# One decode block on one core: load buffers at multiples of 1 KB, w4 loaded in 2 KB runs, and the last row's probabilities spread in other banks

## The chip, the core and the metric

The kernel runs on one core of a Trainium2 chip. The core has five engines with queues of their own: TensorE (PE in the profile, with its weight loads as PEld), VectorE (DVE), ScalarE (ACT), GpSimd (POOL) and SyncE (SP), which here issues nearly all DMAs. Sixteen DMA engines move the data. The metric is the device time of one execution in microseconds (us); less is better.

## The reference

One new token for each of 8 batch rows (`x` is 8 x 512). Attention with 32 query heads over 8 K/V heads of 128 looks at the last 2048 cached positions; an MLP block follows. The token shifts of the block's mixer take in nothing but padding at a sequence length of 1, so w1 and w2 contribute nothing.

```python
q = (x_ln @ wq).reshape(B, 1, 32, 128)                 # 512 -> 4096
k, v = k_cache[:, :, 6144:, :], v_cache[:, :, 6144:, :]  # 2048 positions, each head used by 4 query heads
p = softmax(q . k * 128 ** -0.5)
h = x + (p . v).reshape(B, 1, 4096) @ wo               # 4096 -> 512
u = layernorm(h)                                       # input of the second block
h2 = h + u + gelu(layernorm(u) @ w3) @ w4              # 512 -> 1792 -> 512 (hs is zero for S = 1)
```

In bf16 K and V are 32 MB each; wq and wo are 4 MB each, w3 and w4 1.8 MB each.

## The kernel before, in words

**Loads.** SP issues, in a written order, wq, 16 loads of K and 16 of V (2 MB each, half a batch row: 4 heads x 2048 positions), wo in four parts, w3, and w4 in three parts (`load_k` to `load_w4`, lines 618 to 640; the order is the string of line 643). K and V have three buffers each (`knat`, `vnat`). A K load waits until the transposes of the load three before it are done, a V load until the P x V of the one three before it is done; SP's queue is in order, so a load that waits holds all behind it. In a partition a K or V load is one row of 16 KB, wo has rows of 8 KB, w3 four of 3.5 KB, and w4 pieces of 7, 6 and 1 KB: partition p holds rows 14p to 14p + 13 of w4, and the loads take 7, 6 and 1 of them (`W4_AT`, line 601).

The tiles in SBUF lie one behind the other in the order in which they are declared (lines 103 to 171).

**Attention.** 64 items, 8 per batch row. For each, PE transposes 16 blocks of K into one of two pairs of PSUM banks (`pe_T`, line 315); ScalarE copies the lower half and VectorE the upper half to `kT_sb` (`evict`, lines 323 and 325); PE multiplies with the queries (`pe_QK`, line 335) into `S_ps`, one bank for even rows and one for odd. The order of PE's work is that of the loop at line 517: item p is transposed, then the parts of softmax and P x V of earlier rows that `A_WORK` and `B_WORK` place there, then the product with the queries of item p - 2. `LAG` puts the late parts of row 6 four items later, close before those of row 7.

Per row b the softmax has five parts. `softmax_1` to `softmax_3` find the maximum (line 354 on VectorE, small transposes through the bank `sm`), and ScalarE takes the exponential (line 372). `softmax_4` transposes P and VectorE copies it to `PT_sb` (line 384). Then `widen(b, x)`, for x from 0 to 3, spreads P over 128 columns with one matmul into a bank (line 397) and masks the result into `pT_sb`: on VectorE with one product (line 410), or, for x in `ON_ACT` = (1, 3), on ScalarE with four instructions (line 407). Even x use the bank `o_rows`, odd x an `S_ps` bank that is free (`bank_of`, line 388); both banks are also those of P x V. `softmax_5` adds up the row sums (lines 414 and 416).

`pe_PV` (line 426) multiplies the masked P with half a row of V, first into `o_rows`, then into `S_ps`; ScalarE and VectorE write the result as a high and a low bf16 part (lines 432 and 433). `pe_O` (line 443) brings it to the heads' layout; `oX` and `oW` (lines 453 and 459) scale it into the columns of `oW`.

**The rest.** wo comes in two forms: `pe_wo_row` (line 472) puts 24 of the 32 parts as rows into K's fourth bank, split into a high and a low part by lines 478 and 479 and brought back by `pe_hr` (line 502); meanwhile `pe_wo` (line 493) adds the other 8 parts directly, four matmuls each. A normalisation follows (lines 548 to 556), then 56 matmuls with w3 (line 568: 16, then the matmul for the variance at line 574, then 40), whose weights are columns with a step of 14; a square root and a GELU on ScalarE, each behind a load of its table (lines 581 and 593); 56 matmuls with w4 (line 607) that wait for the three loads in turn; and the sum, a transpose and the store.

`Engine.op` records an instruction with its waits, `emit` writes them to the engine's queue in that order.

Of the kernel before, what the change touches and what calls it, by code (L numbers as in the profile page):

```python
# [6 lines left out]
dt = mybir.dt  # L7
# [13 lines left out]
NC = W // 128  # L21
F = 1792
FC = F // 128
KC = D // 128
EPS = 1e-5

KQ = 4
NQ = 2
NS = 4
# [4 lines left out]
NKT = 4  # L34
LQK = 2
NPB = 3
ON_ACT = (1, 3)
JW = 32
JP = 8
QW = H  # L40


# [30 lines left out]
def bass_sequential_preLN__sliding_block_cached__mixer_s_mlp__decode_kernel(  # L73
# [19 lines left out]
    NITEM = NB * G  # L93
# [3 lines left out]
    with es:  # L97
        sb = lambda shape, dtype, name: es.enter_context(nc.sbuf_tensor(name, shape, dtype))
# [5 lines left out]
        ident_f = sb([128, 128], dt.float32, "ident_f")  # L104
        ident_b = sb([128, 128], dt.bfloat16, "ident_b")
        turn_b = sb([128, 128], dt.bfloat16, "turn_b")
        own_f = sb([128, KQ], dt.float32, "own_f")
        rows_f = sb([128, 64], dt.float32, "rows_f")
        heads_f = sb([128, H], dt.float32, "heads_f")
        sel_l = sb([128, 128], dt.float32, "sel_l")  # L110
        sel_o = sb([128, NS, 64], dt.bfloat16, "sel_o")
        ones_f = sb([128, 128], dt.float32, "ones_f")

        wbig = sb([128, KC * H * DH], dt.bfloat16, "wbig")
        wq_v = wbig[:, :].rearrange("p (k n) -> p k n", k=KC)
# [2 lines left out]
        vnat = sb([128, NV, CQ * DH], dt.bfloat16, "vnat")  # L118
        w3_sb = sb([128, KC, F], dt.bfloat16, "w3_sb")
        w4_sb = sb([128, FC, D], dt.bfloat16, "w4_sb")  # L120
        half = sb([128, B], dt.float32, "half")
        scratch = sb([128, 2], dt.float32, "scratch")
        eps2 = sb([128, 1], dt.float32, "eps2")
# [17 lines left out]
        PT_sb = sb([128, 512], dt.bfloat16, "PT_sb")  # L141
# [33 lines left out]
        kbank = [kT_ps[i // 2][:, (i % 2) * 1024:(i % 2 + 1) * 1024].bitcast(dt.float32) for i in range(4)]  # L175
# [16 lines left out]
        def dma(eng, dst, src, sem, *waits):  # L192
            def f(e):
                e.dma_start(dst, src).then_inc(sem, 16)
            eng.op(f, *waits, inc=False)
# [108 lines left out]
        def V(m):  # L304
            return sem_v[m % NV], 16 * (m // NV + 1)
# [16 lines left out]
        def evict(i):  # L322
            e_lo[i] = AC.op(lambda e: e.activation(kT_sb[:, i % NKT, 0:W // 2], kT_ps[i % 2][:, 0:W // 2], ACT.Copy),  # L323
                            e_Tlo[i], e_QK.get(i - NKT))
            e_hi[i] = DV.op(lambda e: e.tensor_copy(kT_sb[:, i % NKT, W // 2:W], kT_ps[i % 2][:, W // 2:W]),  # L325
                            e_Thi[i], e_QK.get(i - NKT))
# [57 lines left out]
            e_PTs[b] = sm_dv(lambda e: e.tensor_copy(PT_sb[:, :], pT_ps), e_PT[b], e_wide.get((b - 1, KQ - 1)))  # L384

        free = {2: None}

        def bank_of(x):
            if x % 2:
                for at in range(2):  # L390
                    if at in free:
                        return at, S_ps[at]
            return 2, o_rows

        def widen(b, x):
            at, bank = bank_of(x)
            e_wide[b, x] = PE.op(lambda e: e.matmul(bank[:, :], wide[:, x, :], PT_sb[:, :], start=True, stop=True),  # L397
                                 e_PTs[b], free[at], e_wd)
            a = own_f[:, :]
            own = bass.AP(tensor=a.tensor, offset=a.offset, ap=[a.ap[0], [0, KQ], [1, KQ], [0, H]])  # L400
            v = lambda t: t.rearrange("p n (t x) -> p n t x", t=KQ)
            to = v(pT_sb[:, b % 2, :, :].rearrange("p (n x) y -> p x n y", x=KQ)[:, x, :, :])
            got = v(bank[:, :].rearrange("p (n y) -> p n y", n=KQ))
            waits = e_wide[b, x], e_PV.get(NQ * (b - 2) + NQ - 1), e_own
            if x in ON_ACT:
                for t in range(KQ):
                    e = AC.op(lambda e, t=t: e.activation(to[:, :, t, :], got[:, :, t, :], ACT.Copy,  # L407
                                                          scale=own_f[:, t:t + 1]), *waits)
            else:
                e = DV.op(lambda e: e.tensor_tensor(to, got, own, ALU.mult), *waits)  # L410
            e_pT[b, x] = free[at] = e

        def softmax_5(b):
            e_Lb[b] = sm_pe(lambda e: e.matmul(sm[:, LB], sel_l[:, :], lcol[:, b:b + 1], start=True, stop=True),
                            e_exp[b], e_sell)
            e_rL[b] = sm_dv(lambda e: e.reciprocal(rL[:, b:b + 1], sm[:, LB]), e_Lb[b])

        def pe_PV(m):
            b, q = divmod(m, NQ)
            at, bank = bank_of(q)  # L420
            to = (orow, qrow)[m % 2]

            def f(e):
                for n in range(NN):
                    u = n % 2
                    ins = e.matmul(bank[64 * u:64 * (u + 1), :],  # L426
                                   pT_sb[:, b % 2, n, :].rearrange("p (x q) -> p q x", q=NQ)[:, q, :],
                                   vnat[:, m % NV, n * 512:(n + 1) * 512], start=(n < 2), stop=(n >= NN - 2),
                                   tile_position=(0, 64 * u), skip_group_check=True)
                return ins  # L430
            e_PV[m] = PE.op(f, V(m), e_pT[b, KQ - 2], e_pT[b, KQ - 1], free[at])
            e_ohi[m] = AC.op(lambda e: e.activation(to[:, 0, :], bank[:, :], ACT.Copy), e_PV[m], e_O.get(m - 2))  # L432
            e_olo[m] = DV.op(lambda e: e.tensor_tensor(to[:, 1, :], bank[:, :], to[:, 0, :], ALU.subtract), e_ohi[m])  # L433
            free[at] = e_olo[m]
# [27 lines left out]
        hT_ps = S_ps[0]  # L462
        e_wo = []
        hrow = kbank[3]
        LAST = NB - 1
        NP = JW // JP

        def pe_wo_row(k):
            def f(e):
                for j in range(JP * k, JP * (k + 1)):  # L470
                    u = j % 4
                    ins = e.matmul(hrow[32 * u:32 * (u + 1), :], oW[:, j, :], wo_v[:, j, :],
                                   start=(j < 4), stop=(j >= JP * (NP - 1) - 4),
                                   tile_position=(0, 32 * u), skip_group_check=True)
                return ins
            e = PE.op(f, e_oW[LAST], (sem_wo[k], 16), e_hi[NITEM - 1])
            if k == NP - 2:
                e = AC.op(lambda e: e.activation(hr[:, 0, :], hrow, ACT.Copy), e)
                e_wo.append(DV.op(lambda e: e.tensor_tensor(hr[:, 1, :], hrow, hr[:, 0, :], ALU.subtract), e))

# [5 lines left out]
                return ins  # L486
            PE.op(f, free[0], X, e_idb)

        def pe_wo(k):
            def f(e):  # L490
                for j in range(JP * k, JP * (k + 1)):
                    for nb in range(KC):
                        ins = e.matmul(hT_ps[:, nb * B:(nb + 1) * B], wo_v[:, j, nb * 128:(nb + 1) * 128],
                                       oW[:, j, 0:B], start=False, stop=False, skip_group_check=True)
                return ins
            PE.op(f, (sem_wo[k], 16), e_oW[LAST])

        def pe_hr():
            def f(e):
# [10 lines left out]
        def quad(f, q):  # L510
            return lambda b: f(NQ * b + q)
        A_WORK = (((1, softmax_2), (2, softmax_3)), ((0, softmax_1),))
        B_WORK = (((3, softmax_4), (4, each(widen, 0)), (4, each(widen, 1)), (5, each(widen, 2)), (5, each(widen, 3)),
                   (6, softmax_5)),
                  ((6, quad(pe_PV, 0)), (7, quad(pe_PV, 1)), (7, quad(pe_O, 0)), (8, quad(pe_O, 1))))
        LAG = (0, 0, 0, 0, 0, 0, KQ, 0)
        for p in range(NITEM + 24):
            if p < NITEM:
                pe_T(p)
                evict(p)  # L520
            if p == 1:
                e_qblk = q_turn()
            for when in (0, 1):
                for b in range(NB):
                    x = p - (G * b + G - 1 + LQK)
                    for at, part in A_WORK[when]:
                        if x == at:
                            part(b)
                    for at, part in B_WORK[when]:
                        if x == at + LAG[b]:  # L530
                            part(b)
                if when == 0 and 0 <= p - LQK < NITEM:
                    pe_QK(p - LQK)
        pe_x()
        for k in range(NP - 1):
            pe_wo_row(k)
        pe_wo(NP - 1)
        pe_hr()


# [22 lines left out]
        def pe_w3(lo, hi, *waits):  # L563
            def f(e):
                for fc in range(lo, hi):
                    n, f = divmod(fc, FH)
                    for kc in range(KC):
                        ins = e.matmul(y_ps[n][:, f * B:(f + 1) * B],  # L568
                                       w3_sb[:, kc, :].rearrange("p (m k) -> p k m", k=FC)[:, fc, :],
                                       uT[:, kc * B:(kc + 1) * B], start=(kc == 0), stop=(kc == KC - 1))  # L570
                return ins
            return PE.op(f, *waits)
# [25 lines left out]
                                                       ALU.mult, ALU.add), e)  # L598

        z_ps = S_ps[1]  # L600
        W4_AT = (0, 7, 13, FC)
        for n, waits in enumerate(((e_gT[0], free[1]), (e_gT[1],), ())):
            lo, hi = W4_AT[n:n + 2]
            def pe_w4(e, lo=lo, hi=hi):
# [32 lines left out]

        def load_w4(n):
            lo, hi = W4_AT[n:n + 2]
            dma(SP, w4_sb[:, lo:hi, :], B_w4.rearrange("(p k) n -> p k n", k=FC)[:, lo:hi, :], sem_w4[n])  # L640

        turn = {"K": 0, "V": 0, "O": 0}
        for kind in "KQKK" + 9 * "VK" + "VKKVKVKVVOVOVOO":
# [47 lines left out]
```

## Time and profile before

| | |
|---|---|
| median of 3 timed runs | 197.82 us (197.47 to 197.85) |
| the profiled execution | 196.63 us |
| its span, first to last instruction | 195.3 us |
| PE busy, VectorE, ScalarE | 153.8, 94.7, 102.5 us |
| data moved | 79.46 MB, 407 GB/s over the span |
| granted clock of PE, mean | 0.975 |

All rows come from the one profiled execution. Times are from the span's start. In the list of groups a line gives the line of the kernel, engine, operation, tiles, sizes and count, then the busy time in us, the mean of one instruction in ns, and the idle time before them with what ended it. In tables of stretches the columns are: the stretch, its length, busy time (with count) of PE, PEld, DVE, ACT and POOL, the granted clock of PE, the busy share of the DMA engines, and GB/s. "To landing" is the time from the issue of a load to the last of its data. The chain of waits is followed back from the last instruction. Busy time of PE comes from modelled ends of matmuls.

### The profile page before, as it was taken

The numbers are of one execution on the slowest core, as the hardware profiler recorded it, in microseconds if no ns is written. First come the engines' busy times: TensorE is split into PE (matmuls) and PEld (weight loads), VectorE is DVE, ScalarE is ACT, GpSimd is POOL, SyncE is SP. The second block draws the span as 40 slices with busy tenths as digits, with TensorE's granted clock in tenths as the row PEclk, the third lists the DMA queues.
The fourth block names the chain that finished last, engine by engine and source line by source line (L and its number), as shares of the span: only waits on it lengthen the run. The fifth ranks groups of instructions, "written<-read, shape, count | busy, mean of one in ns | idle before, by whom it ended". The sixth has DMA issues, their size and how long they took to land.

```text
span 195.3 us, 4485 instructions
## 1 busy us (share of the span) xinstructions
PE 153.8 (79%) x1997; PEld 105.0 (54%) x2005; DVE 94.7 (48%) x196; ACT 102.5 (52%) x169; POOL 7.7 (4%) x16
## 2 busy tenths in 40 slices
PE   0002989997989798979897986969999997949675
PEld 0001667674657465646564664636766672525475
DVE  7700465654275437543754373527553747251241
ACT  3000568785458545864586355835784686351242
POOL 8300000000000000000000000000000000000012
PEclk9999999999999999999999999999999999997985
DMA  5999999999999999999999999999999999999980
GB/s 223 423 436 426 429 426 429 419 429 423 426 426 421 424 423 429 423 429 426 426 429 423 429 423 426 426 419 429 423 429 423 429 406 436 371 426 412 409 351 31
DMA packets 6370, 79.46 MB, mean 407 GB/s; under 512 B 712, under 2 KB 848, under 8 KB 1616
## 3 DMA queue, kind: packets, MB, share of 16 engines
q1 hardware_dynamic: 6336, 79.18, 96.3%
q8 instruction: 15, 0.25, 0.5%
q14 instruction: 3, 0.02, 0.0%
q10 hardware_dynamic: 16, 0.01, 0.0%
HBM read 79.18 MB, written 0.01 MB: 405 GB/s over the span
## 4 chain that ended last, share of the span: by engine, by line
DMA 51%; PE 37%; DVE 6%; ACT 3%; issue 1%; SPq 1%
DMA knat<-in_A_k_cache_dram 32%; PE kT_ps L315 14%; DMA vnat<-in_A_v_cache_dram 11%; DMA wbig<-in_A_wq_dram 8%; PE o_rows L426 5%; PE S_ps L335 4%; PE S_ps L426 4%; PE S_ps L268 2%; PE kT_ps L568 2%; ACT pT_sb L407 2%; PE S_ps L397 1%; PE sm L443 1%; DVE kT_sb L325 1%; DVE mcol L354 1%; PE S_ps L607 1%
## 5 line engine op out<-in xcount | busy, mean ns | idle before, releaser
L323 ACT ACTIVATE kT_sb<-kT_ps 128x1024 bf16<-128x1024 bf16 x64 | 65.9, 1032 | 32.7 <-PE kT_ps L315 32.5
L315 PE MATMUL kT_ps<-turn_b,knat 128*128 128x128 bf16 x1024 | 68.1, 220 | 10.9 <-DMA knat<-in_A_k_cache_dram 10.9
L315 PEld LDWEIGHTS kT_ps<-turn_b,knat 128*128 128x128 bf16 x1024 | 57.4, 98 | 26.3 <-DMA knat<-in_A_k_cache_dram 14.7
L325 DVE COPY kT_sb<-kT_ps 128x1024 bf16<-128x1024 bf16 x64 | 44.4, 694 | 37.6 <-PE kT_ps L315 36.8
L335 PE MATMUL S_ps<-kT_sb,qblk 128*32 128x512 bf16 x256 | 26.9, 390 | 0.7 <-DVE qblk L290 0.7
L407 ACT ACTIVATE pT_sb<-S_ps,own_f 128x128 bf16<-128x128 f32 x64 | 18.4, 388 | 3.4 <-PE S_ps L397 3.4
L426 PE MATMUL o_rows<-vnat,pT_sb 128*64 128x512 bf16 x128 | 17.0, 412 | 1.2 <-ACT pT_sb L407 1.2
L433 DVE TENSOR_TENSOR orow<-o_rows,orow 128x512 bf16<-128x512 f32 x8 | 5.5, 691 | 20.7 <-ACT orow L432 20.7
L426 PE MATMUL S_ps<-vnat,pT_sb 128*64 128x512 bf16 x128 | 15.3, 382 | 0.2 <-DMA vnat<-in_A_v_cache_dram 0.2
L433 DVE TENSOR_TENSOR qrow<-S_ps,qrow 128x512 bf16<-128x512 f32 x8 | 5.5, 691 | 15.0 <-ACT qrow L432 15.0
L335 PEld LDWEIGHTS S_ps<-kT_sb,qblk 128*32 128x32 bf16 x256 | 7.2, 93 | 9.2 <-issue 4.9
L426 PEld LDWEIGHTS o_rows<-vnat,pT_sb 128*64 128x64 bf16 x128 | 7.2, 117 | 8.2 <-issue 4.0
L432 ACT ACTIVATE orow<-o_rows 128x512 bf16<-128x512 f32 x8 | 4.8, 597 | 13.1 <-PE o_rows L426 13.1
L268 PE MATMUL S_ps<-wbig,xlnT 128*32 128x512 bf16 x32 | 3.6, 629 | 10.1 <-DMA wbig<-in_A_wq_dram 10.1
L432 ACT ACTIVATE qrow<-S_ps 128x512 bf16<-128x512 f32 x8 | 4.8, 597 | 12.7 <-PE S_ps L426 12.7
L410 DVE TENSOR_TENSOR pT_sb<-o_rows,own_f 128x512 bf16<-128x512 f32 x16 | 10.9, 680 | 0.5 <-PE S_ps L335 0.5
L426 PEld LDWEIGHTS S_ps<-vnat,pT_sb 128*64 128x64 bf16 x128 | 6.9, 111 | 7.0 <-issue 1.5
L274 ACT ACTIVATE qrow<-S_ps 128x512 bf16<-128x512 f32 x1 | 0.6, 597 | 17.2 <-PE S_ps L268 17.2
L397 PE MATMUL S_ps<-PT_sb,wide 128*128 128x512 bf16 x16 | 6.1, 381 | 2.3 <-DVE qrow L433 1.0
L268 PEld LDWEIGHTS S_ps<-wbig,xlnT 128*32 128x32 bf16 x32 | 1.2, 138 | 11.6 <-issue 11.6
L594 POOL TENSOR_SCALAR r<-vsum 128x8 f32<-128x8 f32 x1 | 0.2, 243 | 181.9 <-DVE vsum L578 181.9
L372 ACT ACTIVATE P_sb<-S_ps,negcol 128x512 bf16<-128x512 f32 x8 | 5.5, 687 | 2.3 <-DVE negcol L371 2.3
(98 smaller groups left out, 115.7 us busy)
## 6 DMA issues: line engine op xcount, KB each, us to landing
knat<-in_A_k_cache_dram SPq DMA_DIRECT2D x16, 2048.0 KB, 20.3
vnat<-in_A_v_cache_dram SPq DMA_DIRECT2D x16, 2048.0 KB, 20.0
wbig<-in_A_wq_dram SPq DMA_DIRECT2D x1, 4096.0 KB, 16.6
wbig<-in_A_wo_dram SPq DMA_DIRECT2D x4, 1024.0 KB, 15.7
w_sb<-in_B_w_dram SPq DMA_DIRECT2D x1, 1792.0 KB, 17.4
w_sb<-in_B_w_dram SPq DMA_DIRECT2D x1, 896.0 KB, 19.0
w_sb<-in_B_w_dram SPq DMA_DIRECT2D x1, 768.0 KB, 20.5
w_sb<-in_B_w_dram SPq DMA_DIRECT2D x1, 128.0 KB, 19.6
```

Source lines behind the costliest of these rows:

```text
L268: ins = e.matmul(S_ps[j][32 * u:32 * (u + 1), :], xlnT[:, kc, :], wq_v[:, kc, n:n + R * DH], start=(kc == 0), stop=(kc == KC - 1), tile_po ...
L315: ins = e.matmul(kT_ps[i % 2][:, n * 128:(n + 1) * 128], knat[:, j % NK, c * DH:(c + 1) * DH], turn_b[:, :], is_transpose=True)
L323: e_lo[i] = AC.op(lambda e: e.activation(kT_sb[:, i % NKT, 0:W // 2], kT_ps[i % 2][:, 0:W // 2], ACT.Copy), e_Tlo[i], e_QK.get(i - NKT))
L325: e_hi[i] = DV.op(lambda e: e.tensor_copy(kT_sb[:, i % NKT, W // 2:W], kT_ps[i % 2][:, W // 2:W]), e_Thi[i], e_QK.get(i - NKT))
L335: ins = e.matmul(S_ps[b % 2][32 * t:32 * (t + 1), :], qblk[:, b, KQ * q + t, at:at + H], kT_sb[:, i % NKT, :].rearrange("p (n t a) -> p t ...
L372: e_exp[b] = AC.op(lambda e: e.activation(P_sb[:, b % NPB, :], S_ps[j][:, :], ACT.Exp, bias=negcol[:, b:b + 1], scale=1.0, accum_out=lcol[ ...
L397: e_wide[b, x] = PE.op(lambda e: e.matmul(bank[:, :], wide[:, x, :], PT_sb[:, :], start=True, stop=True), e_PTs[b], free[at], e_wd)
L407: e = AC.op(lambda e, t=t: e.activation(to[:, :, t, :], got[:, :, t, :], ACT.Copy, scale=own_f[:, t:t + 1]), *waits)
L410: e = DV.op(lambda e: e.tensor_tensor(to, got, own, ALU.mult), *waits)
L426: ins = e.matmul(bank[64 * u:64 * (u + 1), :], pT_sb[:, b % 2, n, :].rearrange("p (x q) -> p q x", q=NQ)[:, q, :], vnat[:, m % NV, n * 512 ...
L432: e_ohi[m] = AC.op(lambda e: e.activation(to[:, 0, :], bank[:, :], ACT.Copy), e_PV[m], e_O.get(m - 2))
L433: e_olo[m] = DV.op(lambda e: e.tensor_tensor(to[:, 1, :], bank[:, :], to[:, 0, :], ALU.subtract), e_ohi[m])
```

## The change

Four small tiles (`own_f`, `sel_l`, `sel_o`, `ones_f`) are declared behind the load buffers instead of ahead of them. The rows of w4 are dealt out in groups of 256: in group g partition p holds rows 256g + 2p and 256g + 2p + 1, which lie side by side in memory; the three loads take 3, 3 and 1 groups. The columns of w3 are taken in the same order. Of each row's four blocks of P only block 1 is masked on ScalarE. For the last row (b = 7), blocks 0 to 2 go to the first three of K's banks. P x V waits for all four blocks. Before the last row's first P x V, `warm` puts four matmuls whose result nobody reads into K's fourth bank. Of wo, 20 parts instead of 24 go as rows.

```diff
+FG = FC // 2
-ON_ACT = (1, 3)
+ON_ACT = (1,)
+JR = 20
...
-        own_f = sb([128, KQ], dt.float32, "own_f")
-        sel_l = sb([128, 128], dt.float32, "sel_l")
-        sel_o = sb([128, NS, 64], dt.bfloat16, "sel_o")
-        ones_f = sb([128, 128], dt.float32, "ones_f")
         wbig = sb([128, KC * H * DH], dt.bfloat16, "wbig")
...
         w4_sb = sb([128, FC, D], dt.bfloat16, "w4_sb")
+        own_f = sb([128, KQ], dt.float32, "own_f")
+        sel_l = sb([128, 128], dt.float32, "sel_l")
+        sel_o = sb([128, NS, 64], dt.bfloat16, "sel_o")
+        ones_f = sb([128, 128], dt.float32, "ones_f")
...
-        def bank_of(x):
+        LAST = NB - 1
+        def bank_of(x, b=0):
+            if b == LAST and x < KQ - 1:
+                return 3 + x, kbank[x]
             if x % 2:
...
         def widen(b, x):
-            at, bank = bank_of(x)
+            at, bank = bank_of(x, b)
...
+        def warm(b):
+            def f(e):
+                for n in range(4):
+                    ins = e.matmul(kbank[KQ - 1], ident_b[:, :], PT_sb[:, :], start=True, stop=True)
+                return ins
+            if b == LAST:
+                PE.op(f, e_hi[NITEM - 1])
...
-            e_PV[m] = PE.op(f, V(m), e_pT[b, KQ - 2], e_pT[b, KQ - 1], free[at])
+            e_PV[m] = PE.op(f, V(m), *(e_pT[b, x] for x in range(KQ)), free[at])
...
-        def pe_wo_row(k):
+        def pe_wo_row(j0, j1):
             def f(e):
-                for j in range(JP * k, JP * (k + 1)):
+                for j in range(j0, j1):
                     u = j % 4
                     ins = e.matmul(hrow[32 * u:32 * (u + 1), :], oW[:, j, :], wo_v[:, j, :],
-                                   start=(j < 4), stop=(j >= JP * (NP - 1) - 4),
+                                   start=(j < 4), stop=(j >= JR - 4),
...
-                   (6, softmax_5)),
+                   (6, softmax_5), (6, warm)),
...
+            if p == NITEM - 1:
+                free[3], free[4], free[5] = e_lo[p - 1], e_hi[p - 1], e_lo[p]
...
-        for k in range(NP - 1):
-            pe_wo_row(k)
-        pe_wo(NP - 1)
+        for j in range(0, JR, JP):
+            pe_wo_row(j, min(j + JP, JR))
+        pe_wo(JR, NP * JP - JP)
+        pe_wo(NP * JP - JP, NP * JP)
...
-                                       w3_sb[:, kc, :].rearrange("p (m k) -> p k m", k=FC)[:, fc, :],
+                                       w3_sb[:, kc, :].rearrange("p (g m k) -> p g k m", g=FG, k=2)[:, fc // 2, fc % 2, :],
...
-        W4_AT = (0, 7, 13, FC)
+        W4_AT = (0, 6, 12, FC)
...
-            dma(SP, w4_sb[:, lo:hi, :], B_w4.rearrange("(p k) n -> p k n", k=FC)[:, lo:hi, :], sem_w4[n])
+            dma(SP, w4_sb[:, lo:hi, :].rearrange("p (g k) n -> p g (k n)", k=2),
+                B_w4.rearrange("(g p k) n -> p g (k n)", g=FG, k=2)[:, lo // 2:hi // 2, :], sem_w4[n])
```

More of the change, by code (lines that the diff above doesn't have):

```diff
@@ L464, in bass_sequential_preLN__sliding_block_cached__mixer_s_mlp__decode_kernel @@
         hrow = kbank[3]
-        LAST = NB - 1
         NP = JW // JP
-        def pe_wo_row(k):
+        def pe_wo_row(j0, j1):
             def f(e):
-                for j in range(JP * k, JP * (k + 1)):
+                for j in range(j0, j1):
                     u = j % 4
                     ins = e.matmul(hrow[32 * u:32 * (u + 1), :], oW[:, j, :], wo_v[:, j, :],
-                                   start=(j < 4), stop=(j >= JP * (NP - 1) - 4),
+                                   start=(j < 4), stop=(j >= JR - 4),
                                    tile_position=(0, 32 * u), skip_group_check=True)
                 return ins
-            e = PE.op(f, e_oW[LAST], (sem_wo[k], 16), e_hi[NITEM - 1])
-            if k == NP - 2:
+            e = PE.op(f, e_oW[LAST], (sem_wo[j0 // JP], 16), e_hi[NITEM - 1])
+            if j1 == JR:
                 e = AC.op(lambda e: e.activation(hr[:, 0, :], hrow, ACT.Copy), e)
@@ L487, in pe_x, with pe_wo @@
             PE.op(f, free[0], X, e_idb)
-        def pe_wo(k):
+        def pe_wo(j0, j1):
             def f(e):
-                for j in range(JP * k, JP * (k + 1)):
+                for j in range(j0, j1):
                     for nb in range(KC):
@@ L495, in f @@
                 return ins
-            PE.op(f, (sem_wo[k], 16), e_oW[LAST])
+            PE.op(f, (sem_wo[j0 // JP], 16))
         def pe_hr():
```

## The prediction

> **What bounds the kernel now.** I read the page first (span, slices, queues), then the chain of waits in order of time, then the stretches of the last 30 us, then the issues and their landings.
>
> ```profile
> span 195.3 us, 4485 instructions
> DMA  5999999999999999999999999999999999999980
> DMA packets 6370, 79.46 MB, mean 407 GB/s; under 512 B 712, under 2 KB 848, under 8 KB 1616
> q1 hardware_dynamic: 6336, 79.18, 96.3%
> ```
>
> The DMA engines are busy in every slice but the first and the last two. One queue carries 79.18 MB, so the data cannot arrive before about 190 us, whatever the other engines do. The chain (start, length, what) shows where compute still counts:
>
> ```profile
> 127.47 20.97 DMA vnat<-in_A_v_cache_dram
> 148.44 0.04 issue
> 148.48 1.92 PE S_ps L426 x16
> ...
> 163.23 1.15 ACT pT_sb L407 x4
> ...
> 166.52 1.85 PE o_rows L426 x16
> ...
> 171.96 0.41 PE S_ps L397
> 172.37 0.02 issue
> 172.39 1.15 ACT pT_sb L407 x4
> ...
> 174.01 1.15 ACT pT_sb L407 x4
> 175.16 0.14 issue
> 175.30 3.53 PE o_rows L426 x16
> 178.83 1.74 PE S_ps L426 x16
> ...
> 183.46 1.51 PE kT_ps L472 x24
> ...
> 187.68 1.12 PE kT_ps L568 x16
> ...
> 189.11 2.34 PE kT_ps L568 x40
> 191.46 1.58 PE S_ps L607 x56
> 193.04 0.02 issue
> ```
>
> Until 148.48 the chain hangs on loads; from there to the end it is compute alone. But the last loads run close beside it. These are issues of SP (start, length), then single loads (KB each, us from issue to landing), then the group of the four w3 and w4 issues (lengths, first and last start):
>
> ```profile
> 168.40 0.54 SPq L194 DMA_DIRECT2D vnat<-in_A_v_cache_dram  x1
> 170.09 2.78 SPq L194 DMA_DIRECT2D w_sb<-in_B_w_dram  x4
> ```
> ```profile
> vnat<-in_A_v_cache_dram SPq DMA_DIRECT2D x1, 2048.0 KB, 9.5
> w_sb<-in_B_w_dram SPq DMA_DIRECT2D x1, 1792.0 KB, 17.4
> w_sb<-in_B_w_dram SPq DMA_DIRECT2D x1, 128.0 KB, 19.6
> ```
> ```profile
> L194 SPq DMA_DIRECT2D w_sb<-in_B_w_dram x4: 473/532/1114, 170.1 to 172.4; - x4
> ```
>
> The last V lands at 168.40 + 9.5 = 177.9, and its matmuls start at 178.83: 0.9 us to spare. w3 lands at 170.09 + 17.4 = 187.5, and the w3 matmuls start at 187.68: 0.2 to spare. The last 128 KB of w4 land at 172.4 + 19.6 = 192.0; their 4 matmuls are the last of 56 that end at 193.04 with 1.58/56 = 0.028 us each, so they start near 192.8: 0.8 to spare, and the piece before (some 0.3 us earlier, 191.7) is needed after 28 of 56, at 192.25: 0.5 to spare. So compute ends the run, with three loads 0.2 to 0.9 us behind it. A gain in compute alone soon meets a load; a gain in the DMA stream moves everything.
>
> **The load buffers' addresses.** wbig, knat, vnat, w3_sb and w4_sb begin 544 bytes past a multiple of 1 KB in each partition (byte 20000 in the laid-out program) and now begin on one (18432): four small tiles (own_f padded to 32, and three of 512 bytes) are declared behind them. No instruction changes. Per DMA engine there are (6370 - 712)/16 = 354 descriptors with data. What one costs beyond its bytes comes from stretches with different sizes (30 to 150 us: 16 KB rows; 178 to 183: 8 KB and 3.5 KB rows; 18 to 26.5: 16 KB rows, early):
>
> ```profile
> DMA packets 3508, 51.07 MB, mean 426 GB/s; under 512 B 390, under 2 KB 390, under 8 KB 390
> ```
> ```profile
> DMA packets 400, 2.06 MB, mean 412 GB/s; under 512 B 25, under 2 KB 25, under 8 KB 245
> ```
> ```profile
> DMA packets 239, 3.65 MB, mean 430 GB/s; under 512 B 16, under 2 KB 16, under 8 KB 16
> ```
>
> First: 120 us x 16 / 3118 = 615 ns for 16.4 KB. Second: 5 x 16 / 375 = 213 ns for 5.5 KB. The slope is 36.9 ps per byte, which leaves some 10 ns a descriptor (rough, since a stretch cuts packets at its edges). Third: 8.5 x 16 / 223 = 610 ns. So 5 of the 10 ns come and go at unchanged addresses and are not alignment; at most the other 5 can be. Outer bound 354 x 10 ns = 3.5 us gained. Nothing in the rows names a loss, but nothing excludes one either: I allow 2.5 ns the other way, 0.9 us lost. I take half of the 5 ns: 354 x 2.5 = 0.9 us at the end of the stream, 0.8 where w3, V and the last K land. The Trainium skill (DMA: Bandwidth & Descriptors, How a descriptor splits into AXI transactions) has a descriptor that does not start at a multiple of 256 B begin at the boundary below and pay for the unused bytes; 544 past 1 KB is 32 past 256, one 32-byte beat, and by our own slope that estimate is 354 x 1.2 ns = 0.4 us. By that the run would come out at 197.1 instead of the 196.6 below. It also states (Advanced Engine Details and Errata, Clock Domains) that an unobstructed 1 KiB descriptor takes 42 to 43 ns; 1 KB at our slope is 38, so as an estimate 5 of the 10 ns would stay in any case. No run so far shows either.
>
> **w4 in 2 KB runs.** A partition's rows of 7, 6 and 1 KB become 3 + 3 + 1 pieces of 2 KB. Per engine 8 partitions x 3 = 24 descriptors become 56: +32 x 10 ns = 0.3 us, at the end of the stream, with nothing to hide it (bounds: 0 and, at twice the price, 0.6). SP still issues three loads. The chunks become 6, 6 and 2 rows of 128, so the last two land as 768 and 256 KB.
>
> Sum for the stream: the last landing moves from 192.0 to 192.0 - 0.9 + 0.3 = 191.4. The piece before lands 256 KB / 400 GB/s = 0.65 earlier, at 190.75; its 24 matmuls take 24 x 0.028 = 0.7 and end at 191.45; then 8 matmuls, 0.25, and about 0.15 until the result is out: 191.85 instead of 193.04. That is 1.2 us less, if compute is there by then.
>
> **The masks.** Of each row's four blocks, block 3 goes from ScalarE (1.15 us for its four instructions) to VectorE:
>
> ```profile
> L410 DVE TENSOR_TENSOR pT_sb<-o_rows,own_f 128x512 bf16<-128x512 f32 x16 | 10.9, 680 | 0.5 <-PE S_ps L335 0.5
> ```
>
> For rows 0 to 5 this adds 0.68 us to VectorE per row of some 20 us, and the copies of K behind it wait; the loads set the pace there, so I cost it at nothing (without that cover, 0.7 a row). For row 6 it stands on the path. VectorE's queue has mask 2 (to 164.9), now mask 3 (to 165.6), and only then the reduce of Mrow, on which the lcol matmul, the reciprocal and the first P x V of row 6 wait through the shared bank sm. That P x V began at 166.52; it slips by about 0.4. For row 7 the blocks 0 to 2 go to K's banks, idle after the last copy, so they no longer wait for the S bank and for each other: the chain 171.96, 172.39, 173.59, 174.01 goes. Next late is VectorE: mask 0 to 172.9, then oX and oW of row 6 (they follow the O matmuls of row 6, which wait for orow/qrow), then masks 2 and 3, ending near 175.1. Against 175.16 + 0.14 that is 0.15 less in all. PE's new wait on all four blocks ends with the same mask; behind it on PE stands nothing but the rest of the tail. The V load of SP that waits for row 6's first P x V is issued 0.4 later, behind several us of other loads (landing 9.5 us after issue against 4.9 for 2 MB at 426 GB/s): free.
>
> **Four extra matmuls (warm).** The rows of PE's clock (us, busy of PE, PEld, DVE, ACT, POOL, clock, DMA share, GB/s):
>
> ```profile
> 172.00:174.00 2.00, 1.66 (x13) 1.02 (x13) 1.51 (x4) 1.14 (x4) 0.00 (x0) 1.00 1.01 422
> 174.00:176.00 2.00, 0.79 (x5) 0.42 (x7) 0.38 (x2) 1.14 (x4) 0.00 (x0) 0.80 0.94 401
> 176.00:178.00 2.00, 2.00 (x12) 0.99 (x10) 0.00 (x0) 0.00 (x0) 0.00 (x0) 0.50 1.00 422
> ```
>
> Row 7's first P x V runs at half clock: 3.53 us against 1.85 for row 6's. Four matmuls of 512 columns (about 0.9 us) now stand where PE waited for masks. If they hold the clock, that P x V ends 1.7 earlier, at 177.0; but the last V lands at 177.9, less 0.8. So of 1.7 about 1.0 + 0.8 is usable at best, and if the clock falls anyway nothing is lost, since PE waited there.
>
> **wo.** Row form takes 20 instead of 24 (1.51 x 4/24 = 0.25 less); the other form gets 48 matmuls instead of 32, about 1.3 us, under the 1.3 us that ScalarE and VectorE need for the rows' two halves (bounds: 0 and +0.3 outside).
>
> **w3 in steps of 2.** Step 14 cost 1.12/16 = 0.070 and 2.34/40 = 0.058 us a matmul; w4's contiguous weights cost 0.028. What step 2 costs no row shows: between. Only the first 16 matter, since the rest lie beside ScalarE's table load: 0 to 0.65 us less, I take 0.3.
>
> **Sum of the compute side.** Last V lands at 177.9 - 0.8; P x V, wo and norm follow as before, less 0.25, so uT is ready at 187.6 - 1.7 - 0.25 = 185.7 (warm works) or about 186.5 (it does not). w3 lands at 187.5 - 0.8 = 186.7: it decides in both cases, so warm, masks and wo vanish behind it. The w3 matmuls start 1.0 earlier, and w4's, 0.3 more, at 190.15; 24 of them end at 190.8, when the second piece is there (190.75). So the stream ends the run: 191.85, a gain of 1.2 us, of which 0.9 - 0.3 is the stream's own and 0.6 is slack behind w4 that the compute side gives up. The profiled execution took 196.63, below all three timed runs; I subtract from their median: 197.82 - 1.2 = 196.6. The measurement tells 0.2% (0.4 us) from no change.
>
> **Rivals.**
> *Alignment gives nothing.* For it: the rate of 426 GB/s varies with time, not with address. Then the last landing is 192.3, the result 192.75: 0.3 less, 197.5, within 0.2%. Chance 0.19.
> *Alignment gives most of the 10 ns*, say 7. Then 2.5 us of the stream go: the last landing is 189.8, which allows 190.25, 2.8 less. Compute has to follow: the V at 148.44 comes 354 x 148/190 x 7 ns = 1.9 earlier, masks and wo give 0.4, w3's step 0.3, and a clock that falls gives no more: 2.6 less, 195.2. Against it: the 5 ns that vary at fixed addresses. Chance 0.14.
> *w4's small pieces hold the end up.* The 1.8 MB of w4 now take 4.5 us (187.5 to 192.0). In 2 KB pieces they may move at 310 GB/s as against 400: +1.2 us. With no gain from alignment the last landing is 193.2, the result 193.65: 0.6 slower, 198.4. It decides once w4's stretch grows by over 0.6 us more than alignment saves. For it: they are the smallest data descriptors in number; against it: the 10 ns. Chance 0.13, with all other ways to lose.
> *Warm fails.* Half clock again at 176 to 178: as worked out, the time stays within 0.1 of the forecast as long as w3 decides.
>
> **How the numbers follow.** The forecast (alignment saves 0.4 to 2 us of stream) has 0.54 and its own range 195.6 to 197.4. Faster by over 0.2%: 0.54 + 0.14 = 0.68; same 0.19; slower 0.13. The range for 8 in 10 reaches from the large gain to the small loss: 195.1 to 198.2.
>
> **What would show it.** Right: stretch 30 to 150 at 428 GB/s or more; w3 landing before 187, and the w3 matmuls starting with that landing; the w4 matmuls waiting for a load; clock 1.00 at 176 to 178. Wrong: the same 426 GB/s (alignment is nothing), a last w4 landing after 192.5 (the small pieces), PE waiting for a mask beyond 175.5, or w3 matmuls still at 0.06 us.

## The result, and the profile after

Six timed runs of each: 195.67 us median (194.42 to 196.36) against 197.64 (197.18 to 198.29). The ratio is 0.9891 with a 95% interval of 0.9849 to 0.9933: 2.2 us faster. The prediction said 196.6, between 195.1 and 198.2.

The page of the changed kernel, the lines that answer to those shown of before:

```profile
span 194.9 us, 4506 instructions
DMA  5999999999999999999999999999999999799990
DMA packets 6883, 79.47 MB, mean 408 GB/s; under 512 B 712, under 2 KB 720, under 8 KB 2128
q1 hardware_dynamic: 6848, 79.18, 95.9%
```

512 more packets are w4's small pieces. The same bytes move, but one slice of the DMA line near the end, at about 166 to 170.5 us, now shows a gap. The profiled execution (196.35 us) is one of the two longest of the six. Its stretch from 30 to 150 us:

```profile
DMA packets 3538, 51.51 MB, mean 429 GB/s; under 512 B 393, under 2 KB 393, under 8 KB 393
```

120 us x 16 / 3145 = 610.5 ns for a 16 KB descriptor, against 120 x 16 / 3118 = 615.8 before. The chain of waits (start, length, what):

```profile
126.39 20.85 DMA vnat<-in_A_v_cache_dram
147.24 0.04 issue
147.29 1.92 PE S_ps L439 x16
...
165.82 3.55 PE o_rows L439 x16
169.38 0.55 PE sm L382 x4
169.93 0.02 SPq L196
...
172.06 0.60 SPq L196
172.66 0.04 issue
172.71 18.62 DMA w_sb<-in_B_w_dram
191.33 0.04 issue
191.38 1.03 PE S_ps L622 x32
192.41 0.02 issue
```

The V load on which the tail's chain hangs lands at 147.24 instead of 148.44: 1.2 us gained by then. At the end the w4 matmuls wait for a piece of w4, as forecast, but it lands at 191.33 and not at 190.75. But between the two the gain is lost again: row 6's first P x V takes 3.55 us, at half clock, where it took 1.85, and SP's last loads wait for it. Stretches of the changed kernel, columns as before (the clock, the DMA share and GB/s are the last three):

```profile
164.00:166.00 2.00, 1.14 (x6) 0.98 (x8) 1.06 (x5) 0.00 (x0) 0.00 (x0) 0.73 0.96 410
166.00:168.00 2.00, 2.00 (x12) 0.82 (x10) 0.02 (x1) 0.78 (x2) 0.00 (x0) 0.50 0.99 422
168.00:170.00 2.00, 2.00 (x14) 0.75 (x12) 0.00 (x0) 0.58 (x1) 0.00 (x0) 0.50 0.51 209
170.00:172.00 2.00, 2.00 (x12) 0.85 (x12) 1.02 (x2) 0.02 (x1) 0.00 (x0) 0.56 0.79 295
176.00:178.00 2.00, 1.62 (x15) 0.82 (x14) 0.81 (x3) 0.00 (x0) 0.00 (x0) 1.00 0.95 389
```

Between 168 and 172 the DMA engines move 209 and 295 GB/s: they have run dry. Against 429 that is 2 x (220 + 134)/429 = 1.65 us of stream lost. The half clock has moved from row 7 (before: 0.50 at 176 to 178) to row 6.

### The profile page after: what moved, and what is told of

Read it like the earlier page. It is cut to its first block, busy times and chain, and to the rows that moved or that the text cites. A ratio compares the mean times of both kernels' runs of the same rounds, so it can differ in the third digit from the quotient of the medians.

```text
span 194.9 us, 4506 instructions
## 1 busy us (share of the span) xinstructions
PE 155.2 (80%) x2021; PEld 104.1 (53%) x2021; DVE 98.9 (51%) x204; ACT 94.7 (49%) x137; POOL 7.7 (4%) x16
## 4 chain that ended last, share of the span: by engine, by line
DMA 61%; PE 30%; DVE 5%; SPq 2%; issue 1%
DMA knat<-in_A_k_cache_dram 32%; PE kT_ps L317 14%; DMA vnat<-in_A_v_cache_dram 11%; DMA w_sb<-in_B_w_dram 10%; DMA wbig<-in_A_wq_dram 9%; PE S_ps L337 4%; PE o_rows L439 4%; PE S_ps L439 2%; SPq L196 2%; PE S_ps L270 2%; DVE mcol L356 1%; DVE kT_sb L327 1%; PE sm L456 1%; DVE pT_sb L415 1%; DVE qblk L292 1%
## 5 line engine op out<-in xcount | busy, mean ns | idle before, releaser
L439 PE MATMUL S_ps<-vnat,pT_sb 128*64 128x512 bf16 x128 | 16.3, 399 | 0.2 <-DMA vnat<-in_A_v_cache_dram 0.2
L415 DVE TENSOR_TENSOR pT_sb<-o_rows,own_f 128x512 bf16<-128x512 f32 x14 | 9.5, 682 | 0.5 <-PE o_rows L402 0.5
L412 ACT ACTIVATE pT_sb<-S_ps,own_f 128x128 bf16<-128x128 f32 x28 | 8.0, 375 | 1.2 <-PE S_ps L402 1.2
L278 DVE TENSOR_SCALAR qrow<-S_ps 128x512 bf16<-128x512 f32 x1 | 0.7, 691 | 11.7 <-PE S_ps L270 11.7
## 6 DMA issues: line engine op xcount, KB each, us to landing
w_sb<-in_B_w_dram SPq DMA_DIRECT2D x1, 1792.0 KB, 15.2
w_sb<-in_B_w_dram SPq DMA_DIRECT2D x1, 256.0 KB, 16.5
```

The lines of the kernel that those rows point to most:

```text
L439: ins = e.matmul(bank[64 * u:64 * (u + 1), :], pT_sb[:, b % 2, n, :].rearrange("p (x q) -> p q x", q=NQ)[:, q, :], vnat[:, m % NV, n * 512 ...
```

## The experiments

Times are ratios to runs of the kernel before on the same chip, with a 95% interval. Where a profile's execution may not be typical, the spans of all timed executions are named beside it.

**The parts, one at a time.** Alignment alone: the kernel before, with four declarations moved.

```diff
-        own_f = sb([128, KQ], dt.float32, "own_f")   # and sel_l, sel_o, ones_f
...
         w4_sb = sb([128, FC, D], dt.bfloat16, "w4_sb")
+        own_f = sb([128, KQ], dt.float32, "own_f")   # and sel_l, sel_o, ones_f
```

> The kernel before with only the four small tiles moved behind the load buffers, so that these begin at multiples of 1 KB. Theory A (the stream of loads sets the time and alignment shortens it): the stretch 30 to 150 us runs at 429 GB/s or more instead of 426, the last w4 load lands 1.3 to 1.7 us earlier, and the time falls by 1.0 to 1.6 us, since w3 and w4 had only 0.2 to 0.8 us to spare and the compute chain starts from a V load that comes 1.1 us earlier. Theory B (the gain is the tail's compute: masks, warm, w3): the loads land earlier but the time falls by less than 0.5 us.

Measured: 0.9926 (0.9889 to 0.9962), 1.5 us faster (0.8 to 2.2); the median of its spans is 194.25 us, that of the kernel before beside it 196.1. Its stretch from 30 to 150 us, its last load with its issues, and two pieces of its chain:

```profile
DMA packets 3540, 51.51 MB, mean 429 GB/s; under 512 B 395, under 2 KB 395, under 8 KB 395
```
```profile
w_sb<-in_B_w_dram SPq DMA_DIRECT2D x1, 128.0 KB, 18.7
```
```profile
L194 SPq DMA_DIRECT2D w_sb<-in_B_w_dram x4: 444/490/1343, 168.8 to 171.2; - x4
```
```profile
167.09 9.26 DMA vnat<-in_A_v_cache_dram
176.38 1.94 PE S_ps L426 x16
```

The last w4 load lands at 171.2 + 18.7 = 189.9 instead of 192.0: 2.1 us earlier, where 1.3 to 1.7 were expected. In this execution PE waits for the last V (176.4). Theory A holds, and most of the gain, 1.5 of 2.2 us, is alignment's.

Everything but the alignment: the changed kernel with the four declarations back in their old place (the diff above, reversed).

> The changed kernel with the four small tiles put back ahead of the load buffers, so everything but the alignment. Theory A: within 0.5 us of the kernel before (at most the 0.6 us of slack behind w4 is gained, and 0.3 lost to w4's small pieces), 26 to 426 GB/s as before in the stretch 30 to 150. Theory B: 1 to 2 us faster than before, the whole gain. Theory C (a half clock in the tail, by chance of its phase, takes back part of the gain): the single times differ by 1 us or more among themselves, as those of the changed kernel do.

Measured: 0.9952 (0.9923 to 0.9981), about 0.9 us faster; single times 196.30 to 197.64. The stretch 30 to 150 us ran at 425 GB/s. That is more than theory A allowed (0.5) and less than theory B asked for (1 to 2); the interval, 0.4 to 1.5 us, reaches into both. The single times differ by 1.3 us and the profile has the half clock in row 6 (0.50 at 168 to 170), as theory C has it.

Only w4's runs and w3's columns:

```diff
-    w3_sb[:, kc, :].rearrange("p (m k) -> p k m", k=FC)[:, fc, :]
+    w3_sb[:, kc, :].rearrange("p (g m k) -> p g k m", g=FG, k=2)[:, fc // 2, fc % 2, :]
...
-    W4_AT = (0, 7, 13, FC)
+    W4_AT = (0, 6, 12, FC)
...
-    dma(SP, w4_sb[:, lo:hi, :], B_w4.rearrange("(p k) n -> p k n", k=FC)[:, lo:hi, :], sem_w4[n])
+    dma(SP, w4_sb[:, lo:hi, :].rearrange("p (g k) n -> p g (k n)", k=2),
+        B_w4.rearrange("(g p k) n -> p g (k n)", g=FG, k=2)[:, lo // 2:hi // 2, :], sem_w4[n])
```

> The kernel before with only w4 in 2 KB runs and w3's columns in steps of 2. The w3 matmuls take 0.03 us each, not 0.058 to 0.070, so the GELU's path starts 0.6 us earlier; the 32 more descriptors per DMA engine cost about 10 ns each, so the last w4 load lands 0.3 us later. Theory A: the last load decides, 0 to 0.4 us faster. If the stream did not matter: 0.6 to 1.0 us faster.

Measured: 0.9951 (0.9919 to 0.9982). Its w3 matmuls, and its last load with the group of issues:

```profile
L569 PE MATMUL kT_ps<-uT,w_sb x56: 166/166/180, 187.9 to 189.5; 128*128 128x8 bf16 x56
```
```profile
w_sb<-in_B_w_dram SPq DMA_DIRECT2D x1, 256.0 KB, 16.0
```
```profile
L195 SPq DMA_DIRECT2D w_sb<-in_B_w_dram x4: 489/527/4957, 170.2 to 176.4; - x4
```

56 matmuls start within 1.6 us, 0.029 each (the variance matmul among them): a step of 2 costs no more than no step at all. The last load lands at 176.4 + 16.0 = 192.4, 0.4 later than before (0.3 expected). The profiled span is 195.4, no gain over 195.3, as theory A has it; yet over all executions the gain is 1.0 (0.4 to 1.6), which is what was to be expected if the stream did not matter. The spans suggest how: the kernel before has executions at 195.2 to 196.1 and others near 197.0 (17 of the 35 beside these runs at 196.6 to 197.2); this one has eight at 195.0 to 195.8 and four at 196.2 to 196.7. The upper group has the lower mean clock (0.957 to 0.967, against 0.965 to 0.985), and two profiles of it below (32 and 64 bytes) show what it is: half clock in row 6 as well as in row 7. There compute is late for the loads: with 32 bytes w3 lands at 187.5 and its matmuls start at 189.26. A gain of 0.6 us in w3 can then count in full; in the other executions the loads stop it. This is a reading of the spans, and no run separates the two. The forecast was made from an execution of the lower group.

Only the attention's tail:

```diff
-ON_ACT = (1, 3)
+ON_ACT = (1,)
+JR = 20                    # with bank_of, warm, pe_PV's waits, pe_wo_row and pe_wo as in the change
```

> The kernel before with only the edits of the attention's tail: blocks 0, 2 and 3 of every row masked on VectorE, row 7's blocks in K's banks, the four extra matmuls, 20 parts of wo as rows. Theory A: within 0.4 us of the kernel before, as w3's landing (0.2 us to spare) stops what these edits gain. Theory B: 1 us faster or more. Theory C: row 6's first P x V comes 0.4 us later because its fourth mask stands in VectorE's queue ahead of the reduce on which it waits; when a window of little PE work falls there, the clock is halved for rows 6 and 7, V's last load is issued late and the DMA engines run dry: such runs are 0.5 to 1.5 us slower than before.

Measured: 0.997 (0.994 to 1.0001): not clear of no change. The interval, from nothing to 1.2 us, excludes neither theory A (0.4) nor theory B (1), and no execution was slower than the slowest of the kernel before, as theory C had it for some. Of its 12 spans ten lie at 195.3 to 195.7 and the others at 196.2 and 196.6, where the kernel before has half of its executions at 196.6 or more. So these edits may keep executions out of the upper group; the times do not show it.

**With the aligned stream.** The changed kernel again:

> The changed kernel once more, beside the following ones. Theory A+C (alignment speeds the stream up; in some executions row 6's P x V meets a half clock): 1 to 2.5 us faster than before, single times in two groups about 1 to 2 us apart.

0.9876 (0.9842 to 0.9911), 2.5 us faster. The spans (193.3, 193.5, 193.7, 194.2, 194.6, 194.8) do not fall into two groups.

Alignment with w3 and w4, without the tail's edits (both diffs above):

> The kernel before with alignment and with w4 in 2 KB runs and w3 in steps of 2, but without the edits of the attention's tail. If these edits gain nothing because the loads stop them (theory A): as fast as the changed kernel, 2 to 2.5 us faster than before. If they cost something by way of row 6's clock (theory C): faster than the changed kernel by 0.3 us or more. If they are what the last microsecond hangs on (theory B): 0.5 us or more slower than the changed kernel.

0.9865 (0.9826 to 0.9904). As fast as the changed kernel: the tail's edits add nothing that these runs can tell. Nothing speaks for theory B. The intervals reach 0.8 us to each side, too wide to exclude it or theory C; the median of the spans, 193.3 against 193.95, leans to theory C. Its last load:

```profile
w_sb<-in_B_w_dram SPq DMA_DIRECT2D x1, 256.0 KB, 15.5
```
```profile
L195 SPq DMA_DIRECT2D w_sb<-in_B_w_dram x4: 455/512/4774, 168.8 to 174.6; - x4
```

174.6 + 15.5 = 190.1, against 189.9 with alignment alone: w4's small pieces cost 0.2, from one profile of each.

**Row 6's clock.** The old split of the masks for rows 0 to 6:

```diff
-            if x in ON_ACT:
+            if x in (ON_ACT if b == LAST else (1, 3)):
```

> The changed kernel, but rows 0 to 6 have blocks 1 and 3 masked on ScalarE as before; only row 7 has the new split. Theory C: row 6's first P x V starts 0.4 us earlier relative to the last K load, the half clock in rows 6 and 7 becomes rarer, and the median is 0.3 to 1 us better than the changed kernel's. Theory A: no difference over 0.3 us.

0.9866 (0.9834 to 0.9898): no difference that the intervals show. Its profile has the whole clock from 164 to 178.

Three idle matmuls in row 6:

```diff
+        def fill(b):
+            def f(e):
+                for n in range(3):
+                    ins = e.matmul(kbank[KQ - 1], ident_b[:, :], PT_sb[:, :], start=True, stop=True)
+                return ins
+            if b == LAST - 1:
+                PE.op(f, e_hi[NITEM - 1])
...
-                   (6, softmax_5), (6, warm)),
+                   (6, fill), (6, softmax_5), (6, warm)),
```

> The changed kernel with three more matmuls of 512 columns, whose result nobody reads, in row 6, where PE waits for VectorE ahead of the lcol matmul. Theory C: PE's clock stays whole through row 6, and the median is 0.3 to 1 us better than the changed kernel's, its slowest time 1 us better. If the clock does not hang on these gaps: no difference, or 0.2 us slower for the matmuls themselves.

0.9841 (0.9804 to 0.9879); the median of six is 194.41 against 195.33 for the changed kernel beside it. The intervals overlap, so it is not shown to be better. The profile of it has the whole clock in both rows, here row 6:

```profile
166.00:168.00 2.00, 2.00 (x22) 0.95 (x18) 0.00 (x0) 1.12 (x3) 0.00 (x0) 1.00 0.93 393
168.00:170.00 2.00, 2.00 (x24) 1.25 (x20) 1.02 (x2) 0.42 (x2) 0.00 (x0) 1.00 0.87 320
```

and its chain then hangs on the last V, which the prediction named as the bound of what a whole clock can gain:

```profile
167.56 8.90 DMA vnat<-in_A_v_cache_dram
176.50 1.94 PE S_ps L447 x16
```

The profile of the run before it, without these matmuls, has the whole clock in row 6 as well. So one profile of each does not show that the matmuls hold it, and what decides whether row 6's clock falls stays open.

**Which multiple matters.** The kernel before with the tiles moved, and 32, 64, 256 or 512 bytes put back ahead of the load buffers, one execution of each:

```diff
+        own_f = sb([128, KQ], dt.float32, "own_f")     # 32 bytes
+        pad = sb([128, 16], dt.float32, "pad")         # or 64 bytes
+        pad = sb([128, 64], dt.float32, "pad")         # or 256 bytes
+        sel_l = sb([128, 128], dt.float32, "sel_l")    # or 512 bytes
         wbig = sb([128, KC * H * DH], dt.bfloat16, "wbig")
```

> The kernel before with the small tiles behind the load buffers, except own_f, so that the buffers begin 32 bytes past a multiple of 1 KB. If what matters is the start against some power of two of 64 or more: as the kernel before, 425 to 426 GB/s in the stretch 30 to 150 us. If it were the place in memory, or a neighbour: 429 as with alignment.

> The aligned variant of the kernel before (only the small tiles moved), with 64 unused bytes ahead of the load buffers, which so begin at a multiple of 64 and of no more. If a multiple of 64 is enough: 429 GB/s in the stretch 30 to 150 us and a last w4 load near 189.9. If it takes 256 (the rule of the Trainium skill on where a transaction starts) or more: 425 to 426 and near 192.

> The same with 256 unused bytes ahead: a multiple of 256 and of no more. If 256 is enough: 429 GB/s in the stretch 30 to 150 us. If it takes 512 or 1 KB: 425 to 426.

> The same with one of the 512-byte tiles ahead of the load buffers: a multiple of 512 and of no more. If 512 or less is enough: 429 GB/s. If it takes 1 KB, as the change's words have it: 425 to 426.

The stretch 30 to 150 us, in that order:

```profile
DMA packets 3510, 51.10 MB, mean 426 GB/s; under 512 B 390, under 2 KB 390, under 8 KB 390
```
```profile
DMA packets 3511, 51.12 MB, mean 426 GB/s; under 512 B 390, under 2 KB 390, under 8 KB 390
```
```profile
DMA packets 3538, 51.50 MB, mean 429 GB/s; under 512 B 394, under 2 KB 394, under 8 KB 394
```
```profile
DMA packets 3536, 51.46 MB, mean 429 GB/s; under 512 B 394, under 2 KB 394, under 8 KB 394
```

32 and 64 past a multiple of 256 give 426 GB/s, as the kernel before (32 past); a multiple of 256 gives 429, as 1 KB does. So 256 is enough and 64 is not; 128 was not tried. The last w4 load lands at 192.6 and 192.7 with 32 and 64 bytes, at 190.1 and 190.0 with 256 and 512, though the first two also have the half clock in row 6. By the rates the trace agrees with the rule of the Trainium skill (DMA: Bandwidth & Descriptors, How a descriptor splits into AXI transactions) on starts at multiples of 256 B; here it is the destination in SBUF that starts off the multiple. It does not agree with that page's count of extra 32-byte beats: one for 32 bytes and two for 64 are, as an estimate by our slope, 1.2 and 2.4 ns, whereas a descriptor took 615.4 and 615.2 ns, against 610.7 and 611.1 with 256 and 512 bytes. That is over 4 ns more, and no more for 64 than for 32.

The execution with 64 bytes is also one of the upper group of spans (196.9); in its page row 6's slices of the clock line and row 7's are both low:

```profile
PEclk9999999999999999999999996999999998797985
```

The slices of 4.9 us at 162 to 172 carry row 6's drop (8 and 7 in the 34th and 35th place), the one at 177 to 182 (7 in the 37th) row 7's. This kernel has nothing of the tail's edits: row 6's half clock can hit the kernel before as well.

## Why the prediction was right, and where it was off

**What bounds the kernel.** Right in the main: loads lie close behind compute, and a change of the stream moves the time. With alignment alone the last V, w3 and w4 all came earlier. But that w3's landing "decides in both cases" was wrong in the changed kernel's profile: w3 lands at 171.54 + 15.2 = 186.7, as forecast, and its matmuls start 0.7 later, when uT is there (start, length, what, in brackets the idle time before and what ended it):

```profile
187.39 0.56 PE L583 MATMUL kT_ps<-uT,w_sb 128*128 128x8 bf16 x16 [0.29 <-DVE uT L567]
190.46 1.93 PE L622 MATMUL S_ps<-gT,w_sb 128*128 128x8 bf16 x56 [1.27 <-ACT gT L608]
```

A sign of being wrong came true there as well: PE waits for row 7's masks until 176.8, beyond 175.5, since row 6's half clock delays the work ahead of them.

**Alignment.** The mechanism was right, the size was not: the term of 354 x 2.5 ns = 0.9 us should have been about 321 x 5.3 = 1.7, with the descriptors per engine that start after 27 us. With alignment alone the last landing moved by 2.1; the other 0.4 is not explained. In the changed kernel's profile the last piece lands at 175.5 + 16.5 = 192.0, no earlier than before, as the stream loses 1.65 us on the way. The failing step is the sentence that "5 of the 10 ns come and go at unchanged addresses and are not alignment". They were alignment: in the traces' packet records a 16 KB packet that starts at 18 to 26 us takes 611 ns (median) in both kernels, and one at 60 to 150 us takes 614 (mean 619.0) before and 611 (mean 613.9) in the changed kernel. So early on misalignment costs nothing, and aligned loads keep the early rate. The other 5 ns, which the prediction allowed to alignment, largely stayed: 610.5 against 16379 x 36.9 ps = 604.4 ns. When misalignment begins to cost is no fixed time: in the run with the tail's edits alone, at the same addresses, the median packet takes 611 ns from 30 to 46 us, too. Why it begins is open.

**w4 in 2 KB runs.** Right: +0.3 forecast, 0.2 (aligned) and 0.4 (not aligned) measured. The rival's 310 GB/s had no row behind it: a 2 KB packet takes 84 ns aligned and 87 not, which is 390 and 377 GB/s on 16 engines.

**w3.** Taken at 0.3 out of 0 to 0.65; the first 16 matmuls start within 187.39 to 187.8 in the changed kernel, and its 56 in all take a step of 2 like no step:

```profile
L583 PE MATMUL kT_ps<-uT,w_sb x56: 166/166/181, 187.4 to 189.0; 128*128 128x8 bf16 x56
```

From w3's start to w4's the changed kernel takes 190.46 - 187.39 = 3.07 us, before 191.39 - 187.68 = 3.71: 0.64 less, the upper bound. The w4 matmuls now wait for the GELU (the line of 190.46 above), so more is not to be had from w3's step.

**Masks.** The slip of row 6 was right: from the last copy of K to its first P x V 5.56 us (160.26 to 165.82) against 5.08 (161.44 to 166.52). That this was free was wrong in the profiled execution: "behind several us of other loads" and so free counted 0.4 us of delay and a whole clock. With half the clock the last V is issued at 169.42 instead of 168.40, and the engines run dry.

**warm.** Row 7's clock held (1.00 at 176 to 178). That this is warm's doing is likely, not shown by itself: in all six profiles of kernels with warm, row 7's first P x V takes 1.9 us, and in six of the eight without it 3.2 to 3.5, but in the two with alignment alone and with alignment, w3 and w4 it takes 1.9 as well. In the changed kernel's profile this P x V starts at 176.84, 1.5 later than before, so nothing was gained there; where row 6 has the whole clock (the run with three matmuls in row 6) the last V stops the gain, as said. The half clock in row 6 was not foreseen. Among the profiles it comes and goes, with the tail's edits and without, so a forecast from one execution could not place it.

**The sum.** 1.2 us forecast; 2.2 measured (0.67% to 1.51%, 1.3 to 3.0 us). The gain lies nearer to the rival "alignment gives most of the 10 ns" (2.6 us, chance 0.14) than to the forecast, and the stream's term was 0.8 too small. The rest (0.6 of slack and 0.64 of w3) would count in full in executions in which compute is late, and be lost in those in which the loads are; that is read from the spans and not separated by a run. That the total stayed within the range is in part luck: the stream gave more than forecast, and row 6's clock, which was not foreseen, took some back.

## What to carry to other kernels

In a kernel that lives on its loads, look at where the load buffers begin in a partition: a small tile declared ahead of them can put every descriptor off a multiple of 256 bytes, here 0.9% of the rate and 1.5 us of 198. Before a compute edit near the end is priced, subtract each load's landing from its first use; with 0.2 to 0.9 us to spare, an edit of several steps gained by itself nothing that was clear of no change. Where a clock or a queue varies between executions, take the bound from several, not from one profile.

## What was not expected of the hardware

A start in SBUF 32 or 64 bytes past a multiple of 256 costs 4 to 5 ns a descriptor of 16 KB (5.3 in the kernel before), and nothing in the first 27 us of the same run (a median of 611 ns at 18 to 26 us, aligned or not). Weights with a step of 14 columns cost 0.058 to 0.070 us a matmul, with a step of 2 columns 0.029, about the 0.028 of contiguous ones.
